# No all-engine barrier ahead of a one-core kernel's program; ScalarE waits for the constants by a semaphore

## The chip, the cores and the metric

The kernel runs on one core of one Trainium2 chip. The metric is the device time of one execution in microseconds (us). The timed value is about 1.3 us longer than the trace's span (190.83 against 189.5 in the profiled run of the kernel before).

## The reference, cut to what matters

Two linear-attention blocks A and B (sequence S = 2048, width D = 640, 32 heads of 20) work on the same x and are mixed by a gate per row:

```python
qkv = x @ wqkv                                   # for A and for B
phi = lambda t: jnp.where(t > 0, t + 1, jnp.exp(t)) + 1e-6
pq, pk = phi(q), phi(k)
kv  = einsum(pk, v); z = sum(pk)
o   = (pq @ kv) / (pq @ z + 1e-6)
out = g * (o_A @ wo_A) + (1 - g) * (o_B @ wo_B)  # g = sigmoid(x . gate_w)
```

Only the beginning matters here: the projection of K, `x @ wk`, tile by tile of 128 rows, and `phi(K)`, whose exponential runs on ScalarE.

## The kernel before

The kernel records operations, orders them with a small scheduler, and emits each engine's instructions with the waits that its bookkeeping cannot rule out. The emitting loop gives an instruction its waits one after the other, sorted by the planned end of what is waited for:

```python
            o.keep = sorted(keep, key=lambda d: d.end)
...
        for o in self.order:
            eng = engs[o.eng]
            for d in o.keep:
                eng.wait_ge(d.sem, d.count)
            ins = o.fn(eng)
```

Ahead of all this the framework has put a preamble: GpSimd writes four small constants (0.10 us each), and then all five engines meet at a barrier (a drain and semaphore events on each). The change takes them to be there for ScalarE's activations (a zero as bias, for instance). Then come the program's own first operations:

```python
    op("DVE", lambda e: e.memset(ONE[:, :], 1.0), 120.0, outs=[bone], name="one")
    op("POOL", lambda e: e.memset(EPSC[:, :], EPS), 100.0, outs=[beps], name="eps")
...
    dma("ACT", "cst", CST[:, :], cap[:, :], 128 * CW * 2, outs=[bcst])
    dma("ACT", "gw", GW5[:, :], ...)
    for c in range(NC):                # on SyncE: x0, wkA0, x1, wkA1, wkA2, ...
        if c < 2:
            ld_x("SP", c)
        ld_wk("SP", "A", c)
...
    warm(6)                            # six 128x512 matmuls of ONE
    ...
    x_tp(0)                            # transpose x tile 0 on TensorE (needs x0, cst)
    k_step("A", 0, 0, pss[0])          # K of tile 0, block A, first of five steps
    x_tp(1)
    ...
```

A K tile takes two of the eight PSUM banks that the kernel allocates (`PS`, 128x8x512). It is freed by the third of these operations (arguments shortened):

```python
        op("ACT", ... activation(EK, psw(ps, D), ACT.Exp) ...)              # "ke"
        op("DVE", ... tensor_scalar(EK, EK, 1.0, EPS, min, add) ...)        # "kt"
        op("DVE", ... scalar_tensor_tensor(PKt, psw(ps, D), 0.0, EK, max, add) ...)  # "ks"
```

The tiles go in the order A0 and A1, B0 and B1, A2, B2, A3, B3 and so on. A2 is the first to reuse banks: those of A0.

Of the kernel before, what the change touches and what calls it, by code (L numbers as in the profile page):

```python
# [6 lines left out]
ACT = mybir.ActivationFunctionType  # L7
# [9 lines left out]
EPS = 1e-6  # L17
# [57 lines left out]
class Sched:  # L75
# [5 lines left out]
        self.order = []  # L81

    def op(self, eng, fn, cost, ins=(), outs=(), after=(), prio=None, name="", dma=None):
        o = Op(eng, fn, cost, list(ins), list(outs), after, len(self.ops) if prio is None else prio, name, dma)
        self.ops.append(o)
        return o

    def run(self):
        todo = {e: [o for o in self.ops if o.eng == e] for e in self.ENGS}
        at = {e: 700.0 for e in self.ENGS}  # L90
        bus = [0.0]
        live = {}
        left = {}
        for o in self.ops:
            for b in set(o.ins) | set(o.outs):
                if b.pool:
                    left[b] = left.get(b, 0) + 1

        def can(o, t):

            w = t
            if o.behind is not None and o.behind.start is None:
                return None
            for d in o.deps:
                if d.end is None:
                    return None
                w = max(w, d.end + (HOP if d.eng != o.eng or d.dma else 0.0))
            for b in o.outs:
                if b.pool and b.slot is None:
                    got = self.pick(b, w)  # L110
                    if got is None:
                        return None
                    w = max(w, got[0])
            return w

        n = len(self.ops)
        while len(self.order) < n:
            best = None
            for e in self.ENGS:
                cand = todo[e]  # L120
                if not cand:
                    continue
                look = cand[:1] if e == "PE" else cand
                pick = None
                for o in look:
                    w = can(o, at[e])
                    if w is None:
                        continue
                    key = (w if w > at[e] + 1e-6 else at[e], o.prio)
                    if pick is None or key < pick[0]:  # L130
                        pick = (key, o)
                if pick and (best is None or pick[0][0] < best[0][0]):
                    best = (pick[0], pick[1], e)
            if best is None:
                raise RuntimeError("stuck: " + ", ".join(c[0].name for c in todo.values() if c))
            (w, _), o, e = best
            for b in o.outs:
                if b.pool and b.slot is None:
                    self.take(b, w)
            for b in o.outs:  # L140
                o.deps += b.war
            o.start = w
            if o.dma:
                at[e] = w + o.dma[0]
                o.end = max(w + o.dma[0] + 1500.0, bus[0]) + o.dma[1] / o.dma[2]
                bus[0] = o.end
            else:
                o.end = at[e] = w + o.cost
                if e == "PE":
                    o.end += 160.0  # L150
            todo[e].remove(o)
            self.order.append(o)
            for b in set(o.ins) | set(o.outs):
                if b.pool:
                    left[b] -= 1
                    if left[b] == 0:
                        end = max(x.end for x in b.readers + b.writers) + HOP
                        users = list(b.readers) + list(b.writers)
                        pool = self.free[b.pool]
                        for s in range(b.slot, b.slot + b.n):  # L160
                            pool.append((end, s, users))
        self.order.sort(key=lambda o: o.start)
        return max(o.end for o in self.ops)
# [85 lines left out]
        return self._seq[o]  # L249


def body(nc, A_x, A_wqkv, A_wo, B_x, B_wqkv, B_wo, gate_w, out, log=None):
    x = A_x[0]
    wqkv = {"A": A_wqkv, "B": B_wqkv}
    wo = {"A": A_wo, "B": B_wo}
# [62 lines left out]
    EPSC = sb("EPSC", [128, 1], f32)  # L318
# [8 lines left out]
    sch = Sched({"ps": 8, "ek": NEK, "eq": NEQ, "os": NOS})  # L327
    op = sch.op
# [6 lines left out]
    def dma(q, name, dst, src, nbytes, ins=(), outs=(), after=(), issue=450.0, transpose=False, prio=None):  # L335
        def fn(e):
            d = dst() if callable(dst) else dst
            with nc.allow_non_contiguous_dma(reason="layout"):
                return e.dma_start(d, src() if callable(src) else src, transpose=transpose)

        o = op(q, fn, 0.0, ins, outs, after, prio=prio, name=name, dma=(issue, nbytes, 95.0 if transpose else 330.0))
        if loading:
            o.behind = chain.get(q)
            chain[q] = o
        return o
# [17 lines left out]
    bcst, bone, beps, bgwb = Buf("cst"), Buf("one"), Buf("eps"), Buf("gwb")  # L363
    bwq = {X: Buf("wq" + X) for X in XS}
    bwv = {X: Buf("wv" + X) for X in XS}
    bwo = {X: Buf("wo" + X) for X in XS}

    op("DVE", lambda e: e.memset(ONE[:, :], 1.0), 120.0, outs=[bone], name="one")  # L368
    op("POOL", lambda e: e.memset(EPSC[:, :], EPS), 100.0, outs=[beps], name="eps")
    bxo = Buf("xo")  # L370
    op("POOL", lambda e: e.memset(XN[:, :, D : D + 1], 1.0), 200.0, outs=[bxo], name="xones")

# [195 lines left out]
    for t in range(2, NT):  # L568
# [13 lines left out]
        outs=[bgg2],  # L582
        prio=LOW + 52,
        name="gm",
# [9 lines left out]
    for i, X in enumerate(XS):  # L594
        for j in range(NB):
# [9 lines left out]
                outs=[b],  # L605
# [454 lines left out]
def bass_gated_mix__linear_attn_block__linear_attn_block__prompt_kernel(nc, *args):  # L1060
    body(nc, *args)
# [28 lines left out]
```

## Time and profile before

| | before |
|---|---|
| time, median of 6 runs | 191.0 us (190.74 to 191.29) |
| span of the trace | 189.5 us |
| TensorE (PE) busy | 98% of the span |
| first DMA / first matmul | 0.73 / 1.05 us |
| activation table load | 1.81 us, for 1.28 us |

From the profile page of the kernel before: the span, PE's busy time with its share and number of instructions, the granted TensorE clock (40 slices, 9 for 90% or more), and the engines' shares of the chain of work that ended last.

```profile
span 189.5 us, 3195 instructions
...
PE 184.9 (98%) x1245; PEld 108.1 (57%) x1269; DVE 127.4 (67%) x251; ACT 95.6 (50%) x171; POOL 0.4 (0%) x6
...
PEclk9999999999999999999999999999999999999999
...
PE 98%; issue 1%; DVE 0%; DVEq 0%
```

One caution on the clock row: time that no clock record covers is counted as full. In this trace the record begins only at 5.50 us, and the slices before it are shown full all the same. The row says nothing of the first microseconds.

PE is the bottleneck from its first instruction to nearly the last, and the chain hardly leaves it. So the time is: when PE starts, plus its work, plus every stall, plus a tail of about 2.1 us (the last matmul ends at 187.36 of 189.5). ScalarE (ACT) is idle half of the time.

What the barrier does shows in the view of the line that holds the preamble (kernel before; columns: engine, operation, count, duration in ns, first and last start in us; a q after the engine's name means its sequencer):

```profile
L1075 POOLq EVENT_SEMAPHORE  x2: 17/17/17, 0.5 to 0.6; - x2
L1075 SPq DRAIN  x1: 7/7/7, 0.0 to 0.0; - x1
L1075 DVEq DRAIN  x1: 10/10/10, 0.1 to 0.1; - x1
...
L1075 POOLq DRAIN  x1: 184/184/184, 0.3 to 0.3; - x1
...
L1075 PEldq DRAIN  x1: 8/8/8, 0.3 to 0.3; - x1
...
L1075 SPq EVENT_SEMAPHORE  x1: 17/17/17, 0.7 to 0.7; - x1
```

SyncE (SP) is ready at 0.0, VectorE at 0.1, PE at 0.3; they go on at 0.7, because GpSimd has to write its constants and drain first (from 0.2 us on; the drain alone takes 0.18). The timeline of the kernel before (start, duration, engine, line, operation, output<-input, count; in brackets the idle time ahead of it and what ended it):

```profile
0.73 0.37 ACTq L339 DMA_DIRECT2D CST<-kconsts  x1
...
0.73 0.38 SPq L339 DMA_DIRECT2D XN<-in_A_x_dram  x1
...
0.83 0.17 DVE L368 MEMSET ONE<- 128x128 bf16 x1 [0.83 <-PEq L1075]
...
1.05 2.74 PE L425 MATMUL ps<-ONE 128*128 128x512 bf16 x6 [1.05 <-DVE ONE L368]
...
1.81 1.28 ACT L524 ACT_TABLE_LOAD   x1 [1.81 <-issue]
...
3.59 0.74 PE L438 MATMUL ps<-CST,XN 128*128 128x128 bf16 x5
...
8.26 1.30 ACT L524 ACTIVATE EK<-ps 128x640 bf16<-128x640 f32 x2 [5.16 <-PE ps L492]
...
9.36 0.82 DVE L535 SCALAR_TENSOR_TENSOR PKA<-ps,EK 128x640 bf16<-128x640 f32 x1
...
11.05 0.38 PE L491 MATMUL ps<-WKW,XT 128*128 128x512 bf16 x1
```

Read three things here. The table load stands in time that ScalarE has free: PE delivers K tile A0 only at 8.26. The sum of A0 on VectorE ends at 9.36 + 0.82 = 10.18 and frees A0's banks. A2's first matmul is the last line, at 11.05, and PE did not wait for it: there are 0.87 us of slack.

### The profile page before, as it was taken

Reading aid. Unit: us, or ns where it says so; the run is one execution under the profiler, and the core shown is the slowest. Engines: PE = TensorE matmul, PEld = TensorE weight load, DVE = VectorE, ACT = ScalarE, POOL = GpSimd, SP = SyncE. Lnnn points to the kernel's source line nnn. Section 1 sums busy time; section 2 is a strip of 40 time slices with the busy share of each in tenths; the row PEclk is TensorE's granted clock in tenths of the full one; section 3 lists DMA queues with packets and bytes.
Section 4 is the critical chain, followed back from the end, with each engine's and each line's share of the span. In section 5 each row is a group of like instructions: output and inputs, shape, how many; then the busy total and the mean of one; then the engine's idle time right before and its main releaser. Section 6 shows DMA issues by size and latency. Waiting matters only on the chain.

```text
span 189.5 us, 3195 instructions
## 1 busy us (share of the span) xinstructions
PE 184.9 (98%) x1245; PEld 108.1 (57%) x1269; DVE 127.4 (67%) x251; ACT 95.6 (50%) x171; POOL 0.4 (0%) x6
## 2 busy tenths in 40 slices
PE   7999999999999999999999999999999999999995
PEld 3555555555565656655557556655666555555552
DVE  2389888888833546478787689888996935865300
ACT  2256565656554545544584777876624875000112
POOL 0000000000000000000000000000000000000000
PEclk9999999999999999999999999999999999999999
DMA  5979999999014011013010006330020053233312
GB/s 142 310 137 139 196 358 377 364 244 208 13 44 105 0 38 35 0 35 31 7 21 13 3 3 144 109 98 5 0 50 19 24 169 94 73 136 108 107 69 69
DMA packets 29469, 19.42 MB, mean 102 GB/s; under 512 B 17390, under 2 KB 29198, under 8 KB 29454
## 3 DMA queue, kind: packets, MB, share of 16 engines
q1 hardware_dynamic: 29300, 19.17, 39.2%
q8 instruction: 10, 0.16, 0.4%
q10 hardware_dynamic: 154, 0.05, 0.2%
q14 instruction: 5, 0.04, 0.1%
HBM read 9.95 MB, written 2.64 MB: 66 GB/s over the span
## 4 chain that ended last, share of the span: by engine, by line
PE 98%; issue 1%; DVE 0%; DVEq 0%
PE ps L913 23%; PE ps L743 22%; PE ps L620 18%; PE ps L491 18%; PE ps L492 5%; PE ps L621 5%; PE ps L661 2%; PE ps L425 1%; PE ps L697 1%; PE ps L438 1%; PE ps L698 0%; PE ps L826 0%; DVE TSB L957 0%; DVE ONE L368 0%; PE ps L472 0%
## 5 line engine op out<-in xcount | busy, mean ns | idle before, releaser
L491 PE MATMUL ps<-WKW,XT 128*128 128x512 bf16 x154 | 43.1, 380 | 0.0
L760 ACT ACTIVATE EK<-ps 128x512 bf16<-128x512 f32 x40 | 23.9, 599 | 31.3 <-PE ps L743 29.9
L492 PE MATMUL ps<-WKW,XT 128*128 128x128 bf16 (+1 forms) x160 | 35.2, 220 | 0.3
L524 ACT ACTIVATE EK<-ps 128x640 bf16<-128x640 f32 x32 | 22.3, 703 | 12.5 <-PE ps L492 6.1
L491 PEld LDWEIGHTS ps<-WKW,XT 128*128 128x128 bf16 x160 | 15.7, 98 | 19.0 <-issue 0.3
L743 PE MATMUL ps<-XT,WQA 128*128 128x512 bf16 x96 | 24.0, 379 | 0.1
L743 PE MATMUL ps<-XT,WQB 128*128 128x512 bf16 x95 | 23.3, 379 | 0.4 <-issue 0.2
L620 PE MATMUL ps<-XN,PKB 128*128 128x512 bf16 x80 | 23.5, 379 | 0.0
L770 DVE TENSOR_SCALAR EK<-EK 128x512 bf16<-128x512 bf16 x40 | 11.6, 291 | 17.2 <-ACT EK L760 17.0
L620 PE MATMUL ps<-XN,PKA 128*128 128x512 bf16 x78 | 23.1, 379 | 0.1
L621 PE MATMUL ps<-XN,PKA 128*128 128x129 bf16 x80 | 17.6, 220 | 0.1
L621 PE MATMUL ps<-XN,PKB 128*128 128x129 bf16 x80 | 17.6, 220 | 0.0
L913 PE MATMUL ps<-WPA,EX 128*128 128x128 bf16 (+1 forms) x116 | 16.8, 296 | 0.2
L913 PE MATMUL ps<-WPB,PKA 128*128 128x512 bf16 (+1 forms) x118 | 16.4, 298 | 0.1
L743 PEld LDWEIGHTS ps<-XT,WQB 128*128 128x128 bf16 x100 | 10.9, 118 | 8.5 <-issue 0.2
L492 PEld LDWEIGHTS ps<-WKW,XT 128*128 128x128 bf16 x160 | 15.7, 98 | 0.0
L743 PEld LDWEIGHTS ps<-XT,WQA 128*128 128x128 bf16 x100 | 10.6, 117 | 8.1
L527 DVE TENSOR_SCALAR EK<-EK 128x640 bf16<-128x640 bf16 x32 | 10.4, 325 | 7.0 <-ACT EK L524 7.0
L959 ACT ACTIVATE TSB<-ps 128x640 bf16<-128x640 f32 (+1 forms) x4 | 2.7, 677 | 23.9 <-PE ps L913 23.9
L620 PEld LDWEIGHTS ps<-XN,PKA 128*128 128x128 bf16 x80 | 9.4, 117 | 7.9
L620 PEld LDWEIGHTS ps<-XN,PKB 128*128 128x128 bf16 x80 | 9.4, 118 | 7.8
L535 DVE SCALAR_TENSOR_TENSOR PKA<-ps,EK 128x640 bf16<-128x640 f32 x16 | 13.2, 825 | 0.6
(77 smaller groups left out, 231.5 us busy)
## 6 DMA issues: line engine op xcount, KB each, us to landing
out_dram<-TSB SPq DMA_DIRECT2D x15, 160.0 KB, 1.8
XN<-in_A_x_dram SPq DMA_DIRECT2D x1, 2240.0 KB, 9.2
WKW<-in_A_wqkv_dram SPq DMA_DIRECT2D x5, 160.0 KB, 3.5
WKW<-in_B_wqkv_dram SPq DMA_DIRECT2D x5, 160.0 KB, 3.9
WQA<-in_A_wqkv_dram SPq DMA_DIRECT2D x1, 800.0 KB, 10.9
WQB<-in_B_wqkv_dram SPq DMA_DIRECT2D x1, 800.0 KB, 13.6
WVA<-in_A_wqkv_dram SPq DMA_DIRECT2D x1, 800.0 KB, 12.8
WVB<-in_B_wqkv_dram SPq DMA_DIRECT2D x1, 800.0 KB, 14.3
```

What stands on the lines that cost most here:

```text
L491: e.matmul(a[:, 0:512], l, WK[X][:, c, 0:512], start=(c == 0), stop=(c == NC - 1))
L492: return e.matmul(a[:, 512:w], l, WK[X][:, c, 512:w], start=(c == 0), stop=(c == NC - 1))
L524: op("ACT", lambda e: e.activation(EK[:, ek.slot, :], psw(ps, D), ACT.Exp), act_cost(D), ins=[ps] + first, outs=[ek], name="ke")
L527: lambda e: e.tensor_scalar(EK[:, ek.slot, :], EK[:, ek.slot, :], 1.0, EPS, op0=ALU.min, op1=ALU.add),
L535: lambda e: e.scalar_tensor_tensor(PKt[X][:, t, :], psw(ps, D), 0.0, EK[:, ek.slot, :], op0=ALU.max, op1=ALU.add),
L620: e.matmul(a[:, 0:512], l, XN[:, t, 0:512], start=(t == 0), stop=(t == NT - 1))
L621: return e.matmul(a[:, 512 : D + 1], l, XN[:, t, 512 : D + 1], start=(t == 0), stop=(t == NT - 1))
L661: r = e.matmul(PS[0:GR, ps.slot, GR * i : GR * i + GR], WV[X][:, c, lo : lo + GR], gv[:, c, :, lo // 5 : lo // 5 + 24], start=(c == 0), st ...
L743: r = e.matmul(PS[:, ps.slot, :], WQ[X][:, c, g::5], XT[:, c, 512 * b : 512 * b + 512], start=(c == 0), stop=(c == NC - 1),)
L760: lambda e: e.activation(EQ[:, eq.slot, :], PS[:, ps.slot, :], ACT.Exp),
L770: lambda e: e.tensor_scalar(EQ[:, eq.slot, :], EQ[:, eq.slot, :], 1.0, EPS, op0=ALU.min, op1=ALU.add),
L913: r = e.matmul(a[:, l0 - lo : h0 - lo], PQ[X, b][:, g, 128 * (t % 4) : 128 * (t % 4) + 128], WP[X][:, g, l0:h0], start=(X == first and g = ...
```

## The change

Its intent is to let every engine begin at once. The barrier's instructions are taken out of the preamble. The constants, which the barrier had guarded, are to be guarded by a semaphore instead: every activation is made dependent on GpSimd's memset of EPSC, which stands behind the four constants on the same engine. (The scheduler's assumed start time also goes from 700 to 300 ns; the resulting order of instructions is the same on every engine.)

```diff
     def op(self, eng, fn, cost, ins=(), outs=(), after=(), prio=None, name="", dma=None):
+        if eng == "ACT" and dma is None:
+            after = list(after) + self.consts
...
-        at = {e: 700.0 for e in self.ENGS}
+        at = {e: 300.0 for e in self.ENGS}
...
+def no_start_barrier(nc):
+    bb = nc.cur_bb.bb
+    bb.instructions = [i for i in bb.instructions if type(i).__name__ not in ("InstDrain", "InstEventSemaphore")]
+
 def body(nc, ...):
+    no_start_barrier(nc)
...
-    op("POOL", lambda e: e.memset(EPSC[:, :], EPS), 100.0, outs=[beps], name="eps")
+    sch.consts = [op("POOL", lambda e: e.memset(EPSC[:, :], EPS), 100.0, outs=[beps], name="eps")]
```

## The prediction

> **What bounds the kernel.** TensorE. The page's busy table has PE at 98% of a 189.5 us span; the chain of waits that ended last is 98% PE; the clock was granted in full in every slice. Only about 1.05 us before the first matmul, 2.1 us after the last and some 1.4 us of small gaps are not PE work. So what moves PE's start, or stalls PE once, moves the end by as much.
>
> **What the change removes.** The start barrier. In the timeline, SyncE, VectorE and ScalarE are ready at 0.0 to 0.1 us and PE at 0.3; all are released at 0.7, after GpSimd has written four constants and drained (0.3 to 0.5). Before: SyncE's and ScalarE's first DMA at 0.73, VectorE's memset of ONE at 0.83, first warm-up matmul at 1.05. After, I expect them near 0.05, 0.1 and 0.4. PE's next steps depend on these alone: six warm-up matmuls (to about 3.6), x tile 0 (landed 2.6 us after its issue), x tile 1 (3.4 after, at 5.0), then weights. So PE's stream begins about 0.67 us sooner.
>
> **What it adds.** A wait of ScalarE's first activation on GpSimd's EPSC memset, done long before: free in itself. But in the built program the activation's other wait, on PE's first K tile, has become an instruction of its own, and the activation table load, placed right before the first activation, now stands behind it. Before, the load ran at 1.81 for 1.28 us in idle time (first exponential at 8.26). After, it starts only when K tile A0 is done, near 7.6, and the first exponential comes near 8.9 instead of 7.6. [...] Otherwise the order on every engine is the same.
>
> **How much reaches PE** (estimate from the before timeline). A K tile takes two of eight PSUM banks, so four fit. Tile A2 takes A0's banks: A0's last VectorE pass ended at 10.18, A2's first matmul began at 11.05: 0.87 us of slack. With that pass 1.30 us later, and 0.05 for the semaphore, A2 starts at 11.53 on the old scale: PE stalls about 0.5 us. Then it heals: VectorE needs about 1.1 us per tile, PE 1.36; B2's banks come free at 12.6, B2 would start at 12.9. No second stall.
>
> **Sum.** -0.67 + 0.5 = about -0.2 us: 190.9 us, range 190.4 to 191.4. Chances: faster by over 2% 0.01, within 2% 0.98, slower by over 2% 0.01. The table load gives most of the gain back.
>
> **What the profile would show.** Right: no barrier semaphores; first DMA before 0.15, first warm-up near 0.4, first transpose matmul of x near 2.9, not 3.59; table load starting after 7, first exponential 1.3 us later; an idle gap of 0.4 to 0.6 us on PE before A2's first matmul, near 10.4 to 10.9, released by VectorE's sum into PKA; from then on the pattern of before, about 0.2 us earlier. Wrong: table load near 1.2, or no PE gap (then the gain is the whole 0.67, 190.4); first matmul near 1 us.
>
> **What would make it wrong.** First DMAs issued at the very start could land slower, taking back the early issue; a second stall in the K stage would make it slower (191.4 or more); the timed interval may not begin where the trace's span does. The three runs spread over 0.54 us.

A sentence is cut from it. No term of its sum is: -0.67 + 0.5 = about -0.2 us stands as recorded, and the table load's 1.28 us in it is read from the trace of the kernel before.

## The result, and the profile after

| | before | after |
|---|---|---|
| time, median of 6 runs each | 191.0 us | 190.81 us (190.54 to 191.11) |
| span of the trace | 189.5 us | 189.2 us |
| first DMA / first matmul | 0.73 / 1.05 us | 0.00 / 0.39 us |
| activation table load starts | 1.81 us | 7.48 us |
| A2's first matmul | 11.05 us | 10.75 us |

The ratio is 0.999 with a 95% interval of 0.9976 to 1.0005: the same within 2%. Ratios here rest on the means of the fast runs of the same rounds, so they are not quite the ratio of the medians quoted. The range that was predicted, 190.4 to 191.4, also holds the 191.0 of no change at all, so the time alone says little for the prediction; the traces and the experiments have to.

The same lines of the page of the kernel after (it has no clock row; the record gives a mean granted clock of 1.0):

```profile
span 189.2 us, 3185 instructions
...
PE 184.9 (98%) x1245; PEld 107.8 (57%) x1269; DVE 127.3 (67%) x251; ACT 95.6 (51%) x171; POOL 0.3 (0%) x6
...
PE 96%; ACT 1%; issue 1%; DVE 1%; DVEq 0%; ACTq 0%
```

Ten instructions fewer (the barrier's eleven are gone, one semaphore event of ScalarE is new), PE's work the same to 0.1 us. But the chain that ended last now leaves PE: 1% is ACT, 1% DVE. The timeline of the kernel after, where line 533 is the exponential and line 544 the sum:

```profile
0.00 0.39 SPq L348 DMA_DIRECT2D XN<-in_A_x_dram  x1
0.12 0.35 ACTq L348 DMA_DIRECT2D CST<-kconsts  x1
0.17 0.17 DVE L377 MEMSET ONE<- 128x128 bf16 x1 [0.17 <-issue]
...
0.39 2.74 PE L434 MATMUL ps<-ONE 128*128 128x512 bf16 x6 [0.39 <-DVE ONE L377]
...
2.93 0.74 PE L447 MATMUL ps<-CST,XN 128*128 128x128 bf16 x5
...
7.48 1.28 ACT L533 ACT_TABLE_LOAD   x1 [7.48 <-PE ps L501]
...
8.77 1.30 ACT L533 ACTIVATE EK<-ps 128x640 bf16<-128x640 f32 x2
...
10.75 0.39 PE L500 MATMUL ps<-WKW,XT 128*128 128x512 bf16 x1 [0.30 <-DVE PKA L544]
```

PE's work up to K tile A0 comes 0.66 to 0.78 us earlier (first matmul 1.05 to 0.39, A0 done 8.26 to 7.48). Then the table load, no longer ahead of the data but behind it, holds the exponential until 8.77, later than in the kernel before, and PE stands still ahead of A2. The last instruction of VectorE, which the experiments use as the end mark, is this in the kernel before:

```profile
187.47 0.29 DVE L957 CAST TSB<-ps 128x128 bf16<-128x128 f32 x1 [10.04 <-PE ps L913]
```

and this in the kernel after:

```profile
187.18 0.29 DVE L966 CAST TSB<-ps 128x128 bf16<-128x128 f32 x1 [10.04 <-PE ps L922]
```

The chain of waits of the kernel after shows the detour in order of time (start, duration, what):

```profile
7.12 0.21 PE ps L500
7.34 0.07 PE ps L501
...
7.43 0.02 ACTq L232
...
7.48 1.28 ACT L533
...
8.77 0.71 ACT EK L533
...
9.51 0.34 DVE EK L536
...
9.87 0.84 DVE PKA L544
...
10.75 0.39 PE ps L500
```

The third line is the key. It is not an activation but a semaphore event of ScalarE's sequencer, 0.02 us long. In the program before, the first activation had one wait, on PE, and carried it itself (on the line that emits the waits, that trace shows no event of ScalarE in its first 9 us). Now it has two. In the built program they are split: the wait on PE, which the emitting loop gives last, is an instruction of its own, then comes the table load, then the activation with the wait on GpSimd. The trace agrees: the event at 7.43, the load at 7.48. The table load, placed right ahead of the activation, now stands behind the event: the same 1.28 us at 7.48 instead of 1.81.

### The profile page after: what moved, and what is told of

Read it like the earlier page. It is cut to its first block, busy times and chain, and to the rows that moved or that the text cites. A ratio compares the mean times of both kernels' runs of the same rounds, so it can differ in the third digit from the quotient of the medians.

```text
span 189.2 us, 3185 instructions
## 1 busy us (share of the span) xinstructions
PE 184.9 (98%) x1245; PEld 107.8 (57%) x1269; DVE 127.3 (67%) x251; ACT 95.6 (51%) x171; POOL 0.3 (0%) x6
## 4 chain that ended last, share of the span: by engine, by line
PE 96%; ACT 1%; issue 1%; DVE 1%; DVEq 0%; ACTq 0%
PE ps L922 23%; PE ps L752 22%; PE ps L629 18%; PE ps L500 17%; PE ps L630 5%; PE ps L501 5%; PE ps L670 2%; PE ps L434 1%; PE ps L706 1%; ACT L533 1%; PE ps L447 1%; DVE PKA L544 0%; ACT EK L533 0%; PE ps L707 0%; PE ps L835 0%
## 5 line engine op out<-in xcount | busy, mean ns | idle before, releaser
L544 DVE SCALAR_TENSOR_TENSOR PKB<-ps,EK 128x640 bf16<-128x640 f32 x16 | 13.2, 825 | 0.6
```

Of the source, the lines that this page charges most:

```text
L544: lambda e: e.scalar_tensor_tensor(PKt[X][:, t, :], psw(ps, D), 0.0, EK[:, ek.slot, :], op0=ALU.max, op1=ALU.add),
```

## The experiments

The theory (T): the early start is worth about 0.7 us or a little more; the table load behind the wait takes about half a microsecond back, as one stall ahead of A2. Rivals: R1, the early start is worth only the 0.2 us seen and the late table load costs nothing; R2, the late table load costs its whole 1.28 us.

Twelve runs were made, of eight new kernels and of repeats of the kernels before, after and swap_waits, all with correct results. One reading from the traces serves them all. Call the *A0 mark* the moment at which ScalarE's first instruction behind K tile A0 starts, and the *last copy* the start of VectorE's last instruction (187.47 us in the kernel before). What happens ahead of the mark is the start; what happens behind it is stalls and work.

| kernel | barrier | table load | A0 mark | last copy | difference |
|---|---|---|---|---|---|
| before | yes | early | 8.26 | 187.47 | 179.21 |
| before_again | yes | early | 8.47 | 187.69 | 179.22 |
| barrier_swap | yes | early | 8.35 | 187.56 | 179.21 |
| swap_waits | no | early | 7.69 | 186.90 | 179.21 |
| swap_again | no | early | 7.75 | 186.97 | 179.22 |
| swap_ref | no | early | 7.50 | 186.72 | 179.22 |
| swap_delay | no | early, then 0.5 us | 7.56 | 186.78 | 179.22 |
| after | no | late | 7.48 | 187.18 | 179.70 |
| after_again | no | late | 7.51 | 187.21 | 179.70 |
| barrier_late_load | yes | late | 8.63 | 188.33 | 179.70 |
| late_load_delay | no | late, then 0.5 us | 7.75 | 187.93 | 180.18 |
| pe_late | no | early | 8.39 | 187.60 | 179.21 |
| warm5 | no | early | 8.22 | 187.43 | 179.21 |
| dma_late | no | early | 7.38 | 186.76 | 179.38 |

The last column falls into three values, apart from dma_late (see there): 179.21 or 179.22 with the early load, 179.70 with the late one, whether there is a barrier or not, and 180.18 with a late load and half a microsecond more.

### after_again: the changed kernel once more

No edit. It is the reference of the next three, on the same chip.

> The changed kernel unaltered, for the same rounds as the next three. Theory (T): the early start brings PE about 0.75 us by the time of tile B1, and the table load behind the wait for PE's first K tile takes 0.46 us of it back as one stall before tile A2, so about 0.3 us of span and 190.7 to 190.9 us. Rival (R1): the early start is worth only these 0.2 to 0.3 us, because transfers set the pace of the first microseconds, and the late table load costs nothing, ScalarE being idle half the time. Both expect 190.7 to 190.9 us here and the table load near 7.5 us in the profile.

Measured: 190.7 us median (190.41 to 190.94, 6 runs); before, in the same rounds, 191.04 (190.67 to 193.21, 11 runs). The table load came at 7.51. Both as expected.

### swap_waits: the two waits in the other order

```diff
-            o.keep = sorted(keep, key=lambda d: d.end)
+            o.keep = sorted(keep, key=lambda d: (o.eng == "ACT" and d.eng == "POOL", d.end))
```

In the built program the wait on GpSimd now stands alone ahead of the table load, and the wait on PE is on the activation.

> The changed kernel with one difference: the first activation's two waits are given in the other order, so that the one on the constants stands alone ahead of the table load and the one on PE's K tile stays on the activation. T: the table load runs near 1.2 us in idle time, the first exponential comes near 7.5 us, PE has no gap before tile A2 (10.3 instead of 10.75 us), and the span falls by 0.4 to 0.5 us against the changed kernel: 190.3 us timed, about 0.7 us below the kernel before. R1: the table load moves in the profile just the same, but the time stays at 190.8 us, within 0.1 of the changed kernel.

Measured: 190.21 us median (190.05 to 190.45), 0.49 below the changed kernel and 0.83 below the kernel before; ratio to before 0.9945 (0.9905 to 0.9985). The timeline of swap_waits:

```profile
1.24 1.28 ACT L533 ACT_TABLE_LOAD   x1 [1.24 <-POOL XN L380]
...
7.69 1.30 ACT L533 ACTIVATE EK<-ps 128x640 bf16<-128x640 f32 x2 [5.16 <-PE ps L501]
...
10.49 0.38 PE L500 MATMUL ps<-WKW,XT 128*128 128x512 bf16 x1
```

The table load is back in idle time and the exponential follows the data at once. The last line is A2's first matmul, with no idle time ahead of it. R1 expected 190.8 and falls. This version beats the changed kernel in these rounds, and the kernel before in all three sets of rounds in which it ran (each interval of the ratio is below 1), though by less than the 2% that counts as faster.

### barrier_late_load: only the added wait, barrier kept

```diff
 # kernel before
     def op(self, eng, fn, cost, ...):
+        if eng == "ACT" and dma is None:
+            after = list(after) + self.consts
...
-    op("POOL", ... name="eps")
+    sch.consts = [op("POOL", ... name="eps")]
```

> The kernel before, barrier kept, with only the wait of the activations on the constants added, so the table load stands behind the wait for PE's first K tile. T: PE starts at 1.05 us as before, the table load runs at about 8.3 us, tile A2 starts 0.45 to 0.55 us later than in the kernel before (near 11.55 instead of 11.05 us), and the time is 191.4 to 191.5 us, 0.45 to 0.5 above the kernel before. R1: the late table load costs nothing: 191.0 us. Rival (R2), that a late table load costs its whole 1.28 us: 192.3 us.

Measured: 191.48 us median (191.05 to 191.68) against 191.04 before: 0.44 more. The ratio, 1.0009 (0.9971 to 1.0046), doesn't settle it: one run of the kernel before took 193.21 us and pulls its mean up. The timeline of barrier_late_load does settle it:

```profile
8.63 1.28 ACT L526 ACT_TABLE_LOAD   x1 [8.63 <-PE ps L494]
...
9.93 1.30 ACT L526 ACTIVATE EK<-ps 128x640 bf16<-128x640 f32 x2
...
11.90 0.39 PE L493 MATMUL ps<-WKW,XT 128*128 128x512 bf16 x1 [0.36 <-DVE PKA L537]
```

A2 began at 11.90, not near 11.55 as expected: in this execution the A0 mark itself came at 8.63 instead of 8.26 (x tile 1 landed 3.6 instead of 3.4 us after its issue, and PE was still slow: the 128x512 matmul at 5.85 took 0.53 us, where the one at 5.66 of the kernel before took 0.39), which no part of the edit explains. From the mark on, the loss is 179.70 - 179.21 = 0.49 us, as in the changed kernel. So the cost belongs to the added wait, not to the missing barrier. R2 expected 1.28 and falls too.

### late_load_delay and swap_delay: is it a slack?

Both get one more activation of 128x512 ahead of the first exponential; its result is not used.

```diff
+        if (X, t) == ("A", 0):
+            op("ACT", lambda e: e.activation(FF["A"][:, :], psw(ps, D)[:, 0:512], ACT.Exp), 0.0, ins=[ps], outs=[Buf("scr")], name="scr")
         op("ACT", lambda e: e.activation(EK[:, ek.slot, :], psw(ps, D), ACT.Exp), ..., name="ke")
```

late_load_delay is the changed kernel with it, swap_delay the kernel with the waits swapped.

> The changed kernel with one more activation of 128x512 (a scratch result, not used) after PE's first K tile and ahead of the first exponential: ScalarE's chain is later by about 0.5 us more. T: the slack of 0.8 us is already spent by the table load, so the whole extra delay reaches PE: the gap before tile A2 grows from 0.46 to about 0.95 us, and the time is 0.5 us above the changed kernel, 191.3 us. R1: 190.8 us, as ScalarE's delays do not reach PE.

> The kernel with the waits swapped (early table load) plus the same extra 128x512 activation ahead of the first exponential that cost 0.6 us behind a late table load. Theory of a slack (T): ScalarE's chain is 0.5 us later, less than the 0.8 us of slack that tile A2 has, so PE has no gap before A2 and the time equals that of the swapped kernel, 190.2 us within 0.15. Rival (proportional: every delay of ScalarE's chain in the K stage reaches PE): 190.7 us.

Measured: late_load_delay 191.3 us median (191.13 to 191.93), 0.6 above after_again; swap_delay 190.13 (190.06 to 190.31, 5 runs), equal to swap_again's 190.11 in the same rounds. The same delay costs all or nothing. The timeline of late_load_delay:

```profile
7.75 1.28 ACT L534 ACT_TABLE_LOAD   x1 [7.75 <-PE ps L501]
9.04 0.60 ACT L534 ACTIVATE FFA<-ps 128x512 bf16<-128x512 f32 x1
9.54 1.29 ACT L535 ACTIVATE EK<-ps 128x640 bf16<-128x640 f32 x2
...
11.51 0.39 PE L500 MATMUL ps<-WKW,XT 128*128 128x512 bf16 x1 [0.85 <-DVE PKA L546]
```

and that of swap_delay:

```profile
7.56 0.60 ACT L534 ACTIVATE FFA<-ps 128x512 bf16<-128x512 f32 x1 [5.02 <-PE ps L501]
8.05 1.29 ACT L535 ACTIVATE EK<-ps 128x640 bf16<-128x640 f32 x2
...
9.14 0.82 DVE L546 SCALAR_TENSOR_TENSOR PKA<-ps,EK 128x640 bf16<-128x640 f32 x1
...
10.35 0.38 PE L500 MATMUL ps<-WKW,XT 128*128 128x512 bf16 x1
```

The extra activation moves the exponential by 0.50 and 0.49 us (9.54 against 9.04, and 8.05 against 7.56). Behind a late load PE's idle time ahead of A2 is 0.85 and the difference in the table grows from 179.70 to 180.18, by 0.48. With an early load the sum of A0 ends at 9.96, A2's first matmul comes at 10.35 unhindered, and nothing is lost. So the slack is real: the 0.87 us of the kernel before, less some 0.06 from the end of the sum to PE's start (10.69 to 10.75 in the kernel after), leave 0.8 us of delay free; what was added beyond that was paid in full: 1.28 + 0.02 - 0.8 = 0.5.

### barrier_swap and before_again: the controls

barrier_swap is barrier_late_load with the swapped order of waits; before_again is the kernel before, one look.

> The control: the barrier kept, the wait on the constants added, but with the two waits in the other order, so that the table load is early. If the barrier alone is what the early start is worth and the order of the waits alone is what the table load costs, this equals the kernel before: 191.0 us within 0.15, table load near 1.8 us, no gap before tile A2. If the added wait costs something of its own, it is slower.

> The kernel before, unaltered, once more, only to see how its first microseconds vary: PE's first matmul at 1.05 us, K tile A0 done between 8.2 and 8.7 us (8.26 in its first profile, 8.63 in the profile of the kernel with the barrier and the late load), 190.7 to 191.4 us.

Measured: barrier_swap 190.87 us median (190.61 to 191.53) against 190.92 before, ratio 0.9998 (0.9975 to 1.0021), table load at 1.87; before_again 191.03 (one run; first matmul at 1.05 and A0 mark at 8.47, both as expected). The wait on the constants is free by itself; only its effect on the place of the table load costs. And with the barrier kept, the version with swapped waits gains nothing over the kernel before. In the same rounds swap_ref, which differs from barrier_swap only by the barrier and the scheduler's assumed start, took 190.06: by medians, the removal alone is worth 0.81 us. As no instruction in the trace of the kernel before reads the four constants, and the activations that read EPSC have a dependency on it anyway, leaving the added wait out altogether should do the same as swapping it; that version was not run.

### swap_again, dma_late, pe_late: which part of the early start counts

dma_late lets SyncE's first load wait for EPSC; pe_late lets VectorE's memset of ONE, and so PE's warm-up, wait for it. Both have the waits swapped (in both, ScalarE needs no wait on GpSimd of its own any more, as PE's first K tile then implies it; the table load comes at 1.07 and 1.18 us in their traces, and none waits for GpSimd).

```diff
 # dma_late
-        dma(q, "x%d" % t, ..., outs=[bxn[t]])
+        dma(q, "x%d" % t, ..., outs=[bxn[t]], after=sch.consts if t == 0 else ())
 # pe_late
-    op("DVE", lambda e: e.memset(ONE[:, :], 1.0), 120.0, outs=[bone], name="one")
     sch.consts = [op("POOL", ..., name="eps")]
+    op("DVE", lambda e: e.memset(ONE[:, :], 1.0), 120.0, outs=[bone], after=sch.consts, name="one")
```

> The kernel with the two waits in the other order once more, as the reference of the next three on the same chip: 190.2 us, table load near 1.2 us, no gap before tile A2.

> The kernel with the waits swapped, but SyncE's first DMA waits for the constant EPSC, so that all its loads are issued about 0.5 us later while PE's warm-up still starts at 0.39 us. If the transfers set PE's pace (x tile 1 landed at 4.4 to 4.7 us in the runs so far, just when PE asks for it): x tile 1 lands near 5.0 us, PE idles for it, and the time is 0.4 to 0.5 us above the swapped kernel, 190.65 us. Rival, that the early start of PE[...] is what the removal is worth: no more than 0.1 us above it.

> The kernel with the waits swapped, but VectorE's memset of ONE waits for the constant EPSC, so that PE's warm-up begins near 0.75 instead of 0.39 us while the loads are still issued at 0.0. If the transfers set the pace: PE's first transposes come 0.35 us later, but the wait for x tile 1 absorbs it wholly or nearly, and the time is within 0.2 us of the swapped kernel. Rival, that PE's own start sets the pace: 0.35 us or more above it, 190.55 us[...].

Measured in the same rounds: before 191.09 us, swap_again 190.11 (189.84 to 191.1), dma_late 190.64 (190.23 to 192.44), pe_late 190.53 (190.12 to 191.05), all medians. By the medians the delays cost some 0.5 and 0.4 us, but pe_late's runs lie wholly within the range of swap_again's. If the medians are right, my expectation for pe_late, that the transfers would hide it, was wrong. dma_late's median met the expectation, but its trace did not show the wait for x tile 1 that was expected. From the timeline of dma_late (its span begins 0.12 us later than the others', because SyncE's first instruction is no longer a DMA):

```profile
1.28 0.43 SPq L348 DMA_DIRECT2D XN<-in_A_x_dram  x1
...
4.17 0.45 PE L447 MATMUL ps<-CST,XN 128*128 128x128 bf16 x5
```

x tile 1 was issued 0.37 us later on this scale (1.28 against 0.91 in swap_again), yet landed 2.8 us after its issue instead of the 3.5 of the kernel after, and PE was not late for it (A0 mark 7.38). What this trace does show is waits for later transfers: ahead of the mark PE waited twice for weights of block A, 0.29 us until 3.57 and 0.21 us until 5.81 (swap_ref's trace has one such wait, of 0.23), and behind it B's first matmul, at 7.63, came 0.18 us later than PE's usual pace, which makes up the odd difference of 179.38 in the table; the profile names no releaser for this last pause. That profiled run was the fastest of its six (190.23); two others took 192.3 and 192.4 us with a granted clock of 1.0 on record, and neither of those is profiled. In pe_late's trace the mark came at 8.39, 0.64 us after swap_again's 7.75 and so more than the 0.39 us by which the warm-up was delayed: PE was also slow for longer (the 128x512 matmul at 6.18 us still took 0.54, where swap_again's took 0.38 or 0.39 from 5.71 on). The medians of this pair suggest that neither start can be given up, but with such overlap and one trace each that is not shown; how the gain divides between them stays open.

### warm5 and swap_ref: one warm-up matmul fewer

```diff
-    warm(6)
+    warm(5)
```

> The kernel with no barrier and the waits swapped, with five warm-up matmuls instead of six: the first transposes of x come 0.42 us earlier, near 2.5 us, as x tile 0 landed at 2.3. If the later transfers (x tile 1 at 4.3 to 4.7 us, weights A1)[...] set the pace, nothing is gained: 190.2 us within 0.15. If PE's own queue sets the pace, 0.3 to 0.4 us are gained, 189.8 us.

> The kernel with no barrier and the waits swapped, as the reference on the same chip: 190.2 us, 0.8 to 0.9 us below the kernel before.

Measured: warm5 190.15 us median (189.99 to 190.81), swap_ref 190.06 (190.03 to 190.7), before 190.92. Nothing is gained, as expected. But the test was weaker than planned: in warm5's trace the first transposes came at 2.83, only 0.10 us before swap_ref's 2.93 and not near 2.5, as the weight load ahead of them still waited for a DMA until 2.80. In warm5's timeline PE still ran at the slow rate past 6 us; in swap_ref's it was fast from about 3.2. The first lines are warm5's:

```profile
3.57 0.58 PE L500 MATMUL ps<-WKW,XT 128*128 128x512 bf16 x1
...
5.87 0.63 PE L500 MATMUL ps<-WKW,XT 128*128 128x512 bf16 x1
```

and this one is swap_ref's:

```profile
3.71 0.38 PE L500 MATMUL ps<-WKW,XT 128*128 128x512 bf16 x1 [0.25 <-DVE XT L462]
```

The same shape takes 0.58 to 0.63 us or 0.38. The pages don't show this: warm5's row of granted clocks is full in every slice, slow matmuls or not, and swap_ref's page has no such row. The slow rate ended between 2.8 (swap_ref) and about 6.1 us (warm5) after PE's first matmul, an estimate from the durations of the matmuls. What ends it was not shown. It may be PE's clock: in the kernel before, the clock record begins, with 1.0, at 5.50 us, between the 128x512 matmul at 4.38 (0.59 us) and the one at 5.66 (0.39 us). But no record covers the slow stretch, so this stays a guess. That the scatter of this end makes up part of the run-to-run spread is likely, but only argued.

## Why the prediction was right

The prediction was 190.9 us with a range of 190.4 to 191.4; the result was 190.81. Point by point:

- *Where the program is bound.* Right. All stalls and gains at the start reached the end: but for dma_late, the differences between mark and last copy repeat to 0.01 us among kernels with the same delay.
- *The early start.* Expected: first DMA near 0.05, memset near 0.1, first matmul near 0.4, transposes near 2.9. Seen: 0.00, 0.17, 0.39, 2.93. This term was a little too small. The first matmul moved by 0.66 us, but the A0 mark moved from a mean of 8.43 us (four profiled kernels with the barrier) to 7.61 (seven without it and with the same start), 0.82 us; and the medians of the kernel with the swapped waits lie 0.83, 0.98 and 0.86 us below those of before in three sets of rounds. From first matmul to mark the traces take 7.21 to 7.58 us with the barrier and 7.09 to 7.36 without. These overlap, so whether the extra 0.16 us is systematic or luck in when PE's slow rate ended and x tile 1 landed stays open.
- *The table load behind the wait.* Right, from the order of the built program alone: expected start near 7.6, exponential near 8.9; seen 7.48 and 8.77. Every trace shows 1.28 us for the load, and here the exponential follows it by 0.01 us.
- *The stall.* Right: expected 0.5 us, shown as 0.49 by three traces, and shown to be the table load's by moving the load with and without the barrier. It also healed at once: no second stall. One sign missed: the idle gap that the profile shows ahead of A2 is 0.30 us, not 0.4 to 0.6. The ends of matmuls are modelled and overlap the next one's start (in the kernel before, the matmul at 9.15 is given 0.38 us, to 9.53, and the next one starts at 9.36), so the starts are the better measure: A2's first matmul began 0.52 us after the one ahead of it (10.23), where about 0.05 is usual, a loss of 0.47.
- *The sum.* -0.67 + 0.5 = -0.2 was predicted; the traces give -0.82 + 0.49 = -0.33 on average, and the two sets of timed rounds -0.19 and -0.34 (medians). The interval of the first ratio includes 1, so the times of that set alone would not prove a gain; the sum of two opposite effects, each tested separately, does explain it. The total came close although the start was worth more than predicted; the range was wide enough to hold that.

## What to carry to other kernels

A wait is not free only because what it waits for is long done: here a second wait on the first activation split off the one on PE, and the table load between the two started only when the data were there, at 7.48 instead of 1.81 us, for 0.49 us of PE's time. After adding or removing a dependency, look at the first activation in the built program: here the table load belonged ahead of the wait on data, which the order of the waits brought about (1.24 us in swap_waits), and an early dependency too (1.07 in dma_late, 1.18 in pe_late). And an idle engine's delay is measured against the slack of the buffers it frees, not against its idle share: here, in the three delays tried (0.5, 1.3 and 1.8 us), 0.8 us were free and the rest was paid in full.
